# A hand-written plan with other keys, and the bias rows of two heads ahead of the rest in SP's queue

## The chip, the cores and the metric

The kernel runs on one core of one Trainium2 chip. The metric is the device time of one execution in microseconds (us); the time of a kernel is the median over its runs.

## The reference, cut to what matters

Three layers in a row: causal attention with a bias from a running sum, a dense layer that takes the largest of three products, and a layer that sends each token to one of 8 experts. The change touches the schedule of the first, with parts of the second in it.

```python
# attention: batch 4, heads 8, seq 576, head_dim 64
scores = scale * np.matmul(q, k.transpose(0, 1, 3, 2))
cum = np.cumsum(np.maximum(s, 0.0), axis=-1)
bias = -(cum[:, :, :, None] - cum[:, :, None, :])
scores = np.where(causal, -1000000000.0, scores + np.minimum(bias, 0.0))
attn = np.exp(scores - np.max(scores, axis=-1, keepdims=True))
attn = attn / (np.sum(attn, axis=-1, keepdims=True) + 1e-09)
x = np.matmul(attn, v)                       # -> 2304 tokens of 512
# dense: d_ff 768
h = np.maximum(np.maximum(x @ w1, x @ w2), x @ w3)
x = h @ w_out
# experts: 8 of 512 -> 1024 -> 512, the largest logit picks one
e_idx = np.argmax(x @ w_gate + modality_bias[modality_id], axis=1)
out[mask] = gate_w[mask, None] * (np.maximum(x[mask] @ w1[e], 0.0) @ w2[e])
```

## The kernel before, in words

The 32 heads go two by two (16 pairs, four pairs a batch, batch 1 first). Products in fp32 precision are made of parts: an operand is rounded to fp32r (its high part, `hl`, `xh`, `w_h`), what is left over is the low part (`q_b`, `xl`, `w_l`), and PE multiplies high with high and high with low.

What one head needs, in the order of its data:

- SP loads its queries and keys (L358, L359, job `lx`) and two rows of the running sum that PE adds as a bias (`lk`). For heads 0 and 1 these rows are read from the tile in SBUF where they are made (L373); for all others from a copy in DRAM (L375), which the job `rows` writes for all heads by two DMAs (L379).
- ACT rounds keys (L387, `ck`) and queries (L390, `cq`); POOL copies the keys (L393, `kb`) and makes the low parts (L397 `kl`, L400 `ql`). `ck` of heads 3 and 5 runs on POOL, `kl` of head 0 on DVE.
- PE makes the scores in six pieces (L407 and L408, `s`; 448, 320, 192 and 64 columns once each and 288 twice), each in one of 3 PSUM banks. DVE adds the mask and takes the minimum (L416, `mn`), ACT the exponentials (L423, `ex`), into one of 4 buffers.
- PE turns the 15 blocks of 128x128 (L428, `t`, four jobs), each in one of 2 PSUM banks; DVE or ACT copies them out (L433, `cp`).
- For each pair: ACT gathers the sums (L437, `r1`), DVE inverts them (L440, `r2`), PE turns them (L444, `rt`, in one of the same 2 banks), ACT copies them (L448, `rc`), SP writes them to DRAM and reads them back spread over partitions (L451, L456; `rw`, `rr`). PE multiplies by the values (L463, `pv`), DVE scales the result into x (L469, L473).

Between these go jobs of the dense layer. Nine of its weight blocks are loaded (L213, `wl`), decoded from float64 and split (L225 on ACT, `wz`; three steps on DVE, `w1`; a DMA issued by POOL, `wd`; a difference on POOL, `ws`). When a batch is done, its columns are split (L487 on ACT, `xc`; L491 on POOL, `xs`), and PE may do "fill" steps of three matmuls on them (L249 to L251, 288 columns, `f`; 168 steps in all). DVE and ACT copy their results (L502, L504, `fe`). The fills have the largest keys on PE: they run when nothing else can. What is left of them after the last head goes on beside the rest of the dense layer, whose matmuls of the same lines have 384 columns.

The order of all this is written out before the kernel is built: `planned` (L117) holds a list of jobs with estimated durations, buffers and transfer times. It takes for each engine the jobs that can start within `LOOK` = 60 ns of the soonest one, and of these the one with the smallest key; the engine with the earliest such start goes first. The keys come from the table `KEY` (L94): `at(h, what)` is h x T + KEY[what], so T is the distance between two heads. `n * KEY["ds"]` and `n * KEY["dt"]` keep the pieces of one head apart. `ready` is the earliest planned start, `wire` the planned time of a transfer and `land` what is added until its data is there. The jobs are then issued in the order found (`manual_schedule`), and each engine runs its own in that order. All that follows the attention is ordered by the compiler's own scheduler.

The lines that the change and its steps touch (the jobs `lk` of heads 0 and 1 stand in the diff, with key -2e8 + h; `kc` is the key of the split of a finished batch's part c, p being the batch's last pair):

```python
def at(h, what, n=0):
    return h * KEY["T"] + KEY[what] + n
rows = job("rows", rows_out, "SP", 1300, -1e8, after=[s_low_], wire=300)
kc = at(2 * (p - 3 + c) + 1, "xc")
```

Of the kernel before, what the change touches and what calls it, by code (L numbers as in the profile page):

```python
# [16 lines left out]
T = B * S  # L17
# [73 lines left out]
CONV = [(0, 3), (1, 3), (2, 5), (3, 7), (4, 7), (5, 9), (6, 13), (7, 15), (8, 17)]  # L91
W_READY, SET_H = 15000, 24
WIRE_FROM, WIRE_TO, WIRE_SLOW = 1300, 900, 1.0
KEY = {"s3": 262888, "T": 15750, "wl": 29386, "wz": 48740, "w1": 225687, "wd": 68498, "ws": 411529, "lx": 95995, "lv": 209700, "ck": 138477, "kb": -116340, "kl": -53033, "ql": -58361, "s": 115494, "mn": -5610, "ex": 153024, "ds": 361, "t": 18694, "dt": 19213, "cp": -53151, "r1": -208485, "r2": -212716, "rt": 15596, "rc": -242689, "rw": 44183, "pv": -165391, "x": -56845, "xc": 100720, "xs": -74110, "fe": -88191}  # L94
R_MOE1 = (2, 4, 7)
R_MOE2 = (1, 3, 5)

# [84 lines left out]
def fused_kernel(tc, qk, vd, sd, w64, mod, wg, wgt, mb, we, cst, csi, out):  # L182
    nc = tc.nc
    V, A, G, P, SP = nc.vector, nc.scalar, nc.gpsimd, nc.tensor, nc.sync
    top = ExitStack()
    with top:
# [73 lines left out]
        with ExitStack() as es:  # L260

            s3 = xbp.tile([32, 3, S], F32, tag="xb", name="s3")
# [83 lines left out]
            def job(name, run, eng, ns, key, **k):  # L346
                j = Job(run, eng, ns, key, **k)
                jobs.append(j)
                st[name] = j
                return j  # L350

            def at(h, what, n=0):
                return h * KEY["T"] + KEY[what] + n

            def load_x(h):
                p, j = divmod(h, 2)
                x = tl["x", h] = qkp.tile([128, 2, S], F32, name="qk_r", bufs=QR_BUFS)
                SP.dma_start(out=x[64:128, 1], in_=qk[PORD[p], 64:128, 1, j])  # L358
                (SP if h else A).dma_start(out=x[:, 0], in_=qk[PORD[p], :, 0, j])  # L359
                if h == 0:  # L360
                    SP.dma_start(out=mask[:, S - 128:S], in_=cst[:, 256:384])
                    SP.dma_start(out=ident, in_=cst[:, 0:128])

            def k_tile(h):
                if ("k_b", h) not in tl:
                    tl["k_b", h] = qkp.tile([66, S], F32R, name="k_b", bufs=KB_BUFS)
                return tl["k_b", h]

            def load_k(h):
                p, j = divmod(h, 2)  # L370
                k_b = k_tile(h)
                if p == 0:
                    SP.dma_start(out=k_b.bitcast(F32)[64:66], in_=augk.bitcast(F32)[16 * j + PORD[0]:16 * j + PORD[0] + 1])  # L373
                else:
                    SP.dma_start(out=k_b.bitcast(F32)[64:66], in_=dk[PORD[p], :, j])  # L375
# [5 lines left out]
            def values_in(p):  # L381
                v_r = tl["v_r", p] = vp.tile([128, 5, 128], F32, name="v_r")
                SP.dma_start(out=v_r, in_=vd[PORD[p]])

            def k_high(h):
                hl = tl["hl", h] = qkp.tile([128, 2, S], F32R, name="hl", bufs=HL_BUFS)
                (G.tensor_copy if h in CK_POOL else A.copy)(out=hl[64:128, 0], in_=tl["x", h][64:128, 1])  # L387
# [4 lines left out]
            def k_again(h):  # L392
                G.tensor_copy(out=k_tile(h)[0:64], in_=tl["x", h][64:128, 1])  # L393

            def k_low(h):
                hl = tl["hl", h]
                (V if h in KL_DVE else G).tensor_tensor(out=hl[0:64, 0], in0=tl["x", h][64:128, 1], in1=hl.bitcast(F32)[64:128, 0], op=ALU.subtract)  # L397

            def q_low(h):
                G.tensor_tensor(out=qbs[h % QB_N][0:64], in0=tl["x", h][0:64, 0], in1=tl["hl", h].bitcast(F32)[0:64, 1], op=ALU.subtract)  # L400
# [17 lines left out]
            def expo(h, c):  # L418
                p, j = divmod(h, 2)
                if ("l", p) not in tl:  # L420
                    tl["l", p] = ss.tile([128, 2, 5], F32, name="l")
                ec = e_bufs[h % E_N][:, EOFF[c]:EOFF[c] + QC[c][2]]
                A.activation(out=ec, in_=ec, func=ACTF.Exp, bias=tl["mn", h][:, c:c + 1], scale=-1.0, accum_out=tl["l", p][:, j, c:c + 1])  # L423
# [91 lines left out]
            sums_s = a = job("s2", s_sums, "DVE", 1346, -1e9, after=[a])  # L515
            b = job("s3", s_high, "ACT", 575, KEY["s3"], after=[a], ready=4350)
            a = job("s4", s_from, "DVE", 360, -1e9, after=[a], lock=True)
            s_low_ = job("s5", s_low, "DVE", 750, -1e9, after=[a, b], lock=True)
            rows = job("rows", rows_out, "SP", 1300, -1e8, after=[s_low_], wire=300)
            turns, highs = None, []  # L520
            for h in range(2 * NP):
                p, j = divmod(h, 2)
                s_x, s_k, s_h, s_q, s_e = (Slot(n) for n in ("qk", "kb", "hl", "qb", "e"))
                lx = job(("lx", h), lambda h=h: load_x(h), "SP", 1900 if h == 0 else 1130, at(h, "lx") if h > 2 else -1e9 + h, takes=[s_x], ready=750, wire=1700)
                if j == 0:
                    s_v, s_p, done = Slot("vr"), [], []
                    lv = job(("lv", p), lambda p=p: values_in(p), "SP", 430, at(h, "lv") if p else -9e8, takes=[s_v], wire=1300, ready=2000)
                ck = job(("ck", h), lambda h=h: k_high(h), "POOL" if h in CK_POOL else "ACT", 671 if h in CK_POOL else 640, at(h, "ck"), after=[lx], takes=[s_h], uses=[s_x], ready=4350)
                cq = job(("cq", h), lambda h=h: q_high(h), "ACT", 600, at(h, "ck", 1), after=[lx, ck], uses=[s_x, s_h])
                if h > 1:  # L530
                    lk = job(("lk", h), lambda h=h: load_k(h), "SP", 300 if h > 1 else 450, at(h, "lx", 1) if h > 1 else -2e8 + h, after=[rows], takes=[s_k], wire=100)
                kb = job(("kb", h), lambda h=h: k_again(h), "POOL", 657, at(h, "kb"), after=[lx, lk] if h > 1 else [lx], takes=[s_k] if h < 2 else [], uses=[s_x, s_k])
                if h < 2:
                    lk = job(("lk", h), lambda h=h: load_k(h), "SP", 300 if h > 1 else 450, at(h, "lx", 1) if h > 1 else -2e8 + h, after=[kb, s_low_], uses=[s_k], wire=100)
                kl = job(("kl", h), lambda h=h: k_low(h), "DVE" if h in KL_DVE else "POOL", 850 if h in KL_DVE else 1415, at(h, "kl"), after=[ck], uses=[s_x, s_h], lock=h in KL_DVE, tail=10 if h in KL_DVE else 0)
                ql = job(("ql", h), lambda h=h: q_low(h), "POOL", 1410, at(h, "ql"), after=[cq], takes=[s_q], uses=[s_x, s_h])
                ex = {}
                for n, (c, k) in enumerate(C_ORDER):
# [3 lines left out]
                    if k or c < 4:  # L542
                        ex[c] = job(("ex", h, c), lambda h=h, c=c: expo(h, c), "ACT", EXP_NS[c], at(h, "ex", n * KEY["ds"]), after=[a], uses=[s_e], tail=0)
                done += ex.values()
# [312 lines left out]
        for w in range(NW):  # L857
# [25 lines left out]
            for i in range(MW // 128):  # L883
                t = w * (MW // 128) + i
# [82 lines left out]
        at = unp.tile([128, U + 1], F32, name="at")  # L967
# [98 lines left out]
```

## Time and profile before

| | |
|---|---|
| median of 3 runs | 734.62 us (733.42 to 736.4) |
| the profiled execution | 734.0 us, its span 732.2 us |
| PE busy | 708.2 us, 97% |
| DVE busy | 497.4 us, 68% |
| ACT busy | 399.9 us, 55% |
| POOL busy | 225.3 us, 31% |

The span runs from the first to the last instruction; 1.8 us of the execution lie around it. PE's matmuls are pipelined and their ends are modelled, so the busy time of PE says that work was in it, not that it ran at its peak. The attention takes the first 210 us or so, and fills and the dense layer overlap its end; the shares above are means over stages with different limits.

### The profile page before, as it was taken

To read this page: it belongs to the slowest core of one execution; us is meant where nothing else is said; L and a number is where in the kernel's file an instruction comes from. 1 tells how busy PE (TensorE), PEld (TensorE's weight loads), DVE (VectorE), ACT (ScalarE), POOL (GpSimd) and SP (SyncE) were. 2 spreads that over 40 slices of the span, in tenths; PEclk is the share of its full clock that TensorE was granted. 3 is DMA by queue.
4 is the path that set the end of the run, shared out by engine and by line. 5 is a ranking of instruction groups with operands and counts; after the bars stand their busy time and mean duration, and the time that the engine had idled before them with its cause. 6 is when DMAs were issued, how large, how long until landed. Compare 5 with 4: busy or idle time off the path is not lost. (4 is left out here: it accounts for less than half of the span.)

```text
span 732.2 us, 13634 instructions
## 1 busy us (share of the span) xinstructions
PE 708.2 (97%) x4602; PEld 633.5 (87%) x4602; DVE 497.4 (68%) x1542; ACT 399.9 (55%) x984; POOL 225.3 (31%) x235
## 2 busy tenths in 40 slices
PE   4899999999999999999999999999999999999996
PEld 3677788878899899899999898999889988999884
DVE  5999787978667932673959796747775665565640
ACT  6899989898644511222222322636564765566631
POOL 8789868776101300010010101041421222212101
PEclk9999999999999999999999999999999999999999
DMA  7476666655236400101001101767567666666600
GB/s 214 144 219 188 203 184 212 190 151 147 81 127 209 164 26 6 49 1 31 36 23 54 52 21 51 258 159 247 153 214 265 225 208 220 212 224 226 222 35 19
DMA packets 43535, 103.83 MB, mean 142 GB/s; under 512 B 9472, under 2 KB 13472, under 8 KB 43456
## 3 DMA queue, kind: packets, MB, share of 16 engines
q1 hardware_dynamic: 35808, 86.04, 37.6%
q0 software_dynamic: 4912, 11.82, 5.1%
q10 hardware_dynamic: 2736, 5.01, 1.9%
q8 instruction: 38, 0.62, 0.4%
q14 instruction: 41, 0.34, 0.2%
HBM read 88.83 MB, written 12.18 MB: 138 GB/s over the span
## 5 line engine op out<-in xcount | busy, mean ns | idle before, releaser
L249 PE MATMUL a_ps<-xh,w_h 128*128 128x384 f32 (+2 forms) x492 | 159.4, 325 | 1.9 <-DVE h L504 1.1
L251 PE MATMUL a_ps<-xh,w_l 128*128 128x384 f32 (+2 forms) x492 | 155.8, 318 | 0.0
L250 PE MATMUL a_ps<-xl,w_h 128*128 128x384 f32 (+2 forms) x492 | 155.7, 317 | 0.0
L768 DVE TENSOR_TENSOR e_l<-e_raw,e_h 128x512 fp32r<-128x512 f32 x160 | 103.9, 689 | 13.5 <-ACT e_h L767 12.1
L767 ACT CAST e_h<-e_raw 128x512 fp32r<-128x512 f32 x160 | 92.9, 622 | 15.9 <-DMA e_raw<-in_we 6.9
L249 PEld LDWEIGHTS a_ps<-xh,w_h 128*128 128x128 f32 x492 | 92.6, 188 | 3.8 <-DVE h L504 1.4
L423 ACT ACTIVATE e<-e,mn 128x448 f32<-128x448 f32 (+4 forms) x160 | 88.6, 557 | 8.5 <-DVE mn L416 8.1
L250 PEld LDWEIGHTS a_ps<-xl,w_h 128*128 128x128 f32 x492 | 92.7, 188 | 0.3
L676 POOL DMA_INDIRECT table<-meta,si x18 | 19.6, 1088 | 238.1 <-DVE nm L664 83.2
L251 PEld LDWEIGHTS a_ps<-xh,w_l 128*128 128x128 f32 x492 | 92.4, 188 | 0.1
L798 PE MATMUL h_ps<-x2t,e_h 128*128 128x256 f32 x288 | 81.0, 282 | 0.0
L799 PE MATMUL h_ps<-x2t,e_l 128*128 128x256 f32 x288 | 80.9, 282 | 0.0
L797 PE MATMUL h_ps<-x2t,e_h 128*128 128x256 f32 x288 | 80.5, 282 | 0.0
L651 DVE CUSTOM_DVE_ANT_0 junk<-x,wg 128x512 bf16<-128x512 f32 x96 | 65.8, 686 | 17.2 <-ACT x L729 16.3
L407 PE MATMUL s_ps<-hl 128*128 128x288 f32 (+1 forms) x192 | 66.0, 354 | 9.9 <-DVE hl L397 6.9
L428 PE MATMUL t_ps<-ident,e 128*128 128x128 f32 x480 | 70.1, 280 | 1.4 <-DVE pt L433 0.6
L416 DVE CUSTOM_DVE_ANT_0 e<-s_ps,mask 128x288 f32<-128x288 f32 (+4 forms) x160 | 63.4, 424 | 9.5 <-PE s_ps L408 9.1
L827 PE MATMUL y_ps<-e_h,gh 128*128 128x512 f32 x152 | 61.5, 405 | 0.4 <-ACT gh L819 0.4
L408 PE MATMUL s_ps<-k_b,q_b 66*128 66x288 f32 (+1 forms) x192 | 57.9, 317 | 4.1 <-DMA k_b<-augk 3.9
L428 PEld LDWEIGHTS t_ps<-ident,e 128*128 128x128 f32 x480 | 56.0, 143 | 5.7 <-DVE pt L433 2.0
L829 PE MATMUL y_ps<-e_h,gl 128*128 128x512 f32 x152 | 60.7, 400 | 0.0
L828 PE MATMUL y_ps<-e_l,gh 128*128 128x512 f32 x152 | 60.0, 395 | 0.0
(179 smaller groups left out, 1484.0 us busy)
## 6 DMA issues: line engine op xcount, KB each, us to landing
e_raw<-in_we SPq DMA_DIRECT2D x80, 512.0 KB
w_raw<-in_w SPq DMA_DIRECT2D x24, 512.0 KB
qk_r<-in_qk SPq DMA_DIRECT2D x31, 288.0 KB
v_r<-in_vd SPq DMA_DIRECT2D x16, 320.0 KB
rb<-r_d SPq DMA_DIRECT2D x32, 160.0 KB
qk_r<-in_qk SPq DMA_DIRECT2D x32, 144.0 KB
x2d<-x ACTq DMA_DIRECT2D x18, 256.0 KB
w_h<-w_z POOLq DMA_DIRECT2D x9, 256.0 KB, 3.9
```

Of the source, the lines that this page charges most:

```text
L249: P.matmul(a_ps, wh[:, c], xh, start=c == 0, stop=False)
L250: P.matmul(a_ps, wh[:, c], xl, start=False, stop=False)
L251: P.matmul(a_ps, wl[:, c], xh, start=False, stop=c == 3)
L407: P.matmul(s_ps, hl[:, 1, q0:q0 + 128], hl[:, 0, k0:k0 + n], start=True, stop=False)
L423: A.activation(out=ec, in_=ec, func=ACTF.Exp, bias=tl["mn", h][:, c:c + 1], scale=-1.0, accum_out=tl["l", p][:, j, c:c + 1])
L428: P.transpose(out=t_ps[:, n * 128:(n + 1) * 128], in_=e_bufs[h % E_N][:, EOFF[c] + kb * 128:EOFF[c] + (kb + 1) * 128], identity=ident)
L651: V.tensor_tensor_reduce(out=junk, in0=x2, in1=wg_sb[ei // 2][:, ei % 2, :], scale=1.0, scalar=0.0, op0=ALU.mult, op1=ALU.add, accum_out=l ...
L767: A.copy(out=h, in_=raw[:, a])
L768: V.tensor_tensor(out=lo, in0=raw[:, a], in1=h.bitcast(F32), op=ALU.subtract)
L797: P.matmul(h_ps, w(hs, f, c), xt[:, 0, c], start=c == 0, stop=False)
L798: P.matmul(h_ps, w(hs, f, c), xt[:, 1, c], start=False, stop=False)
L799: P.matmul(h_ps, w(ls, f, c), xt[:, 0, c], start=False, stop=c == 3)
```

## The change

The diff is three lines. The first gives `KEY` other numbers (a result of a search by annealing, with other weights in what it looks for). The second lets the two writes of all heads' rows to DRAM start at 8500 ns of the plan at the earliest. The third adds 700 ns to the planned landing of the rows of heads 0 and 1. No instruction is added, removed or changed; the order on the engines and queues may differ.

```diff
-KEY = {"s3": 262888, "T": 15750, "wl": 29386, "wz": 48740, "w1": 225687, "wd": 68498, "ws": 411529, "lx": 95995, "lv": 209700, "ck": 138477, "kb": -116340, "kl": -53033, "ql": -58361, "s": 115494, "mn": -5610, "ex": 153024, "ds": 361, "t": 18694, "dt": 19213, "cp": -53151, "r1": -208485, "r2": -212716, "rt": 15596, "rc": -242689, "rw": 44183, "pv": -165391, "x": -56845, "xc": 100720, "xs": -74110, "fe": -88191}
+KEY = {"s3": -97664, "T": 7000, "wl": 40053, "wz": -18589, "w1": 32737, "wd": -43995, "ws": 98173, "lx": -66595, "lv": -5637, "ck": -4681, "kb": -52279, "kl": 21128, "ql": 9680, "s": -4267, "mn": -4185, "ex": 13414, "ds": 50, "t": 10767, "dt": 50, "cp": -42063, "r1": -6337, "r2": -61094, "rt": -71579, "rc": 7287, "rw": -3704, "pv": -70498, "x": -40039, "xc": 39659, "xs": -51512, "fe": 6144}
...
-            rows = job("rows", rows_out, "SP", 1300, -1e8, after=[s_low_], wire=300)
+            rows = job("rows", rows_out, "SP", 1300, -1e8, after=[s_low_], wire=300, ready=8500)
...
-                    lk = job(("lk", h), lambda h=h: load_k(h), "SP", 300 if h > 1 else 450, at(h, "lx", 1) if h > 1 else -2e8 + h, after=[kb, s_low_], uses=[s_k], wire=100)
+                    lk = job(("lk", h), lambda h=h: load_k(h), "SP", 300 if h > 1 else 450, at(h, "lx", 1) if h > 1 else -2e8 + h, after=[kb, s_low_], uses=[s_k], wire=100, land=700)
```

## Rows read from the trace of the kernel before

**Rows 1.** Windows: start:end and length, each engine's busy us, granted clock, DMA.

```profile
core 0: us, PE busy (x) PEld busy (x) DVE busy (x) ACT busy (x) POOL busy (x), PEclk, DMA share, GB/s
20.00:40.00 20.00, 17.54 (x123) 13.71 (x121) 18.97 (x63) 16.87 (x53) 16.70 (x15) 1.00 0.50 140
40.00:80.00 40.00, 38.79 (x290) 30.44 (x290) 36.69 (x124) 38.72 (x114) 34.67 (x33) 1.00 0.73 208
...
40.00:80.00 40.00, 14.01 (x96) 10.50 (x94) 1.00 0.73 208
```

The last of these rows is the same view of line L428 alone.

**Rows 2.** PE by shape, 20 to 80 us: count, busy us, mean ns, idle before.

```profile
L428 PE MATMUL t_ps<-ident,e 128*128 128x128 f32 x144 | 21.7, 280 | 1.3 <-DVE pt L433 0.6 <-ACT r_t L448 0.5
...
L463 PE MATMUL o_ps<-pt,v_r 128*64 128x512 f32 x20 | 5.4, 618 | 0.0
L407 PE MATMUL s_ps<-hl 128*128 128x448 f32 x11 | 4.7, 423 | 0.0
...
L249 PE MATMUL a_ps<-xh,w_h 128*128 128x288 f32 x7 | 2.1, 295 | 0.0
```

**Rows 3.** Timeline of PE, 190 to 222 us: start us, us, instruction, count.

```profile
191.24 0.47 PE L407 MATMUL s_ps<-hl 128*128 128x448 f32 x1
...
191.75 0.30 PE L407 MATMUL s_ps<-hl 128*128 128x288 f32 x1
...
192.05 0.39 PE L407 MATMUL s_ps<-hl 128*128 128x320 f32 x1
...
192.43 0.30 PE L249 MATMUL a_ps<-xh,w_h 128*128 128x288 f32 x1
...
192.83 1.04 PE L428 MATMUL t_ps<-ident,e 128*128 128x128 f32 x8
193.63 0.34 PE L407 MATMUL s_ps<-hl 128*128 128x192 f32 x1
...
194.07 0.38 PE L249 MATMUL a_ps<-xh,w_h 128*128 128x288 f32 x1
...
209.63 2.81 PE L463 MATMUL o_ps<-pt,v_r 128*64 128x512 f32 x20
...
212.49 0.41 PE L249 MATMUL a_ps<-xh,w_h 128*128 128x288 f32 x1
```

**Rows 4.** Timeline, SP's issues of the bias rows.

```profile
8.04 0.75 SPq L373 DMA_DIRECT2D k_b<-augk  x1
...
8.84 1.31 SPq L379 DMA_DIRECT2D dk<-augk  x2
...
10.20 0.64 SPq L373 DMA_DIRECT2D k_b<-augk  x1
```

**Rows 5.** Timeline, the first bias matmuls of heads 0 and 1.

```profile
11.42 0.58 PE L408 MATMUL s_ps<-k_b,q_b 66*128 66x288 f32 x1 [3.89 <-DMA k_b<-augk]
...
14.82 0.44 PE L408 MATMUL s_ps<-k_b,q_b 66*128 66x288 f32 x1
```

**Rows 6.** Timeline, head 3: its queries on ACT and POOL, its first matmul.

```profile
21.88 0.66 ACT L390 CAST hl<-qk_r 128x576 fp32r<-128x576 f32 x1
...
22.61 1.42 POOL L400 TENSOR_TENSOR q_b<-qk_r,hl 64x576 fp32r<-64x576 f32 x1 [4.74 <-ACT hl L390]
...
24.48 0.38 PE L407 MATMUL s_ps<-hl 128*128 128x288 f32 x1
```

**Rows 7.** Timeline, PE and its weight loads around a change of their duration.

```profile
16.82 1.91 PE L428 MATMUL t_ps<-ident,e 128*128 128x128 f32 x8
...
20.14 0.33 PEld L408 LDWEIGHTS s_ps<-k_b,q_b 66*128 66x128 f32 x1
...
20.96 0.19 PEld L407 LDWEIGHTS s_ps<-hl 128*128 128x128 f32 x1
```

**Rows 8.** Fill steps: by shape 205 to 300, window of L249 alone, timeline of ACT.

```profile
L249 PE MATMUL a_ps<-xh,w_h 128*128 128x288 f32 x104 | 31.8, 306 | 1.8 <-DVE h L504 1.1 <-ACT h L502 0.7
...
20.00:100.00 80.00, 5.78 (x19) 3.60 (x19) 1.00 0.65 186
...
72.31 0.77 ACT L487 CAST xh<-x 128x288 fp32r<-128x288 f32 x2
```

## The prediction, made before the result was known

> **What bounds the kernel now.** I read the windows first [rows 1], then the PE rows by shape in the stretch that looked short of work [rows 2], then single rows of the order of time [rows 3 to 7]. The busy column says that PE is nearly always busy, but that column counts each matmul until its modelled end, so I counted work instead: the time from one start to the next where PE is fed without a break [rows 3]. There one head's scores are 0.81 us (191.24 to 192.05: the shapes of 448 and 288 columns, with the small turn of a pair's sums in it), 0.30 for the second 288 (as 191.75 to 192.05), 0.38 for 320 (192.05 to 192.43) and 0.44 for 192 and 64 (193.63 to 194.07): 1.93 us. Eight transposes are 0.80 us (192.83 to 193.63), so the 15 of a head are 1.50. The values of a pair are 2.86 us (209.63 to 212.49), 1.43 a head. One fill step (three matmuls of the MoE layer on a finished half batch) is 0.40 us (192.43 to 192.83). A head is thus 4.86 us of PE.
>
> From 20 to 80 us PE did [rows 2] 11 heads of scores (the shape of 448 columns comes once a head), 144 transposes, 5 pairs of values (that of 512 columns comes four times a pair) and 7 fill steps: 21.2 + 14.4 + 14.3 + 2.8 = 52.7 of 60 us. PE lacks 7.3 us of work there. What is short is not PE: from 40 to 80 us ACT is busy 38.72 of 40 us, with 96 transposes, 6.4 heads, which makes 6.0 us of ACT a head; from 20 to 40 us DVE is busy 18.97 of 20 and ACT 16.87 [rows 1]. Fill steps are the cure, but they need a finished pair, so there are few: 19 by 100 us [rows 8]. After the last head's transposes at about 209 us PE has fills in stock, 104 of 168 steps start after 205 us, and all their waits there make 1.8 us, for the DVE and ACT copies of their results [rows 8]. So an order that feeds PE early takes fills out of that tail one for one, and an order that merely ends the heads sooner is worth nothing. From 260 us on nothing in the code is changed. The whole stock to be won is therefore 7.3 + 1.8, about 9 us of 732, and a bad order can cost as much.
>
> **The change, part by part.** No instruction is added or removed. The planner picks, among jobs that can start within 60 ns of the soonest one on an engine, the one with the lowest key; a job's key is head x T + its offset. Divided by T, the offsets say how many heads one kind of job may be ahead of another.
>
> 1. ACT, conversion against exponentials. Before, the query conversion of head 3 has key 3 x 15750 + 138477 + 1 = 185,728, behind the exponentials of heads 0, 1 and 2 (153,024, 168,774, 184,524). After, it has 3 x 7000 - 4681 + 1 = 16,320, behind head 0's (13,414) and ahead of head 1's (20,414). In general conversions go from level with the exponentials to 2 heads in front (offsets 8.8 against 9.7 heads before, -0.7 against 1.9 after). The row of it: ACT converts head 3's queries at 21.88, POOL had waited 4.74 us for that, and PE's first matmul of head 3 is at 24.48 [rows 6]. It will come some 4 to 5 us sooner. Worth between 0 and those 4.7 us. I take 1.0: DVE must take the minimum of those scores, and it has 20 - 18.97 = 1.03 us free from 20 to 40 us [rows 1], so that is the nearer row.
>
> 2. PE, transposes against scores. Before, every transpose goes ahead of any ready score (offsets 1.2 to 4.8 heads against 7.3). After, scores of heads up to 2 further on go ahead (1.54 against -0.61). Running ahead, 1.34 us of ACT (two conversions of some 0.67, as [rows 6] has one at 0.66) opens 1.93 us of PE. At the average of a head, 6.0 us of ACT for 4.86 of PE, 1.34 us of ACT opens only 1.09. Each head of lead is so worth 0.84 us, and two of them 1.7, once, and only while PE is short. It is bounded by 0 (the three buffers of converted operands or the four score buffers don't allow more lead) and 2 x 1.93 = 3.9 (ACT has the time anyway). I take 1.7: ACT at 38.72 of 40 hasn't the time.
>
> 3. ACT, preparing the fills. The split of a finished batch's columns for the fills (xc) had a key below the exponentials of all heads from 4 on (7 x 15750 + 100,720 = 210,970 for the fourth part); after, 7 x 7000 + 39,659 = 88,659, it stands behind the exponentials up to head 10 (83,414). In the trace two such splits run at 72.31 [rows 8], where ACT, at 6.0 us a head from about 16 us on, is near head 9 or 10 (an estimate). So it comes a head or so later, 6.0 us, while PE lacks 7.3 / 60 = 12%: 0.7 us lost. Bounds: 0, and all 19 steps by 100 us gone, 7.6 us. I take 0.7, since nearly all the steps still find room before the heads end.
>
> 4. The copy of the turned sums (rc) falls from 15 heads ahead of everything on ACT to about one ahead of its own head's exponentials, behind one or two conversions, 0.7 to 1.3 us; it holds one of two transpose banks meanwhile, and the reciprocals' way through DRAM starts that much later. PE has scores to run, so 0; without that cover 16 pairs x 0.7 = 11. The weight conversions' steps on DVE now go ahead of minima some 5 heads on instead of 15; those heads come past 60 us, where most are done: 0, bounded by one such step (0.7 us) either way.
>
> 5. The bias rows. The row asked first, head 0's, is issued at 8.04 behind its producer either way; PE waits for its landing until 11.42. `ready=8500` lets head 1's row, issued at 10.20 behind the two writes at 8.84 (1.31 us), go in front: some 1.3 us sooner [rows 4]. But head 1's first bias matmul runs at 14.82, right behind head 0's last one [rows 5], so 0 is gained; that queue of scores is the cover, and without it the row would be worth at most 1.3. The two writes, and the loads of heads 3 and 4 queued behind them on SP, move by the 0.6 us of the issue at most; head 2's rows are read from what they write. Bounded by 0.6 us lost, taken as 0, since head 3's operands already lay waiting for ACT [rows 6]. `land=700` changes only the plan: it then puts head 0's first full scores 0.7 us later, which is nearer the trace. It has no device time of its own.
>
> The sum: -1.0 - 1.7 + 0.7 = -2.0 us. The profiled execution is 734.0 us with a span of 732.2; so 732.0 for it, and as the median of the runs is 0.6 above it, **732.6 us**.
>
> **The clock of PE.** A weight load takes 0.33 us at 20.14 and 0.19 at 20.96, which are the levels of 1.2 and 2.4 GHz, although the granted clock of that stretch reads 1.00 [rows 1, 7]. Ahead of the rise PE did scores, then from 16.82 transposes among scores [rows 7]. "TensorE: Matmul & The Clock Gate" (the Trainium skill, Part 4: PE-mode transpose) says that transposes don't count as activity for that clock. By that rule scores in front of transposes would bring the rise forward; it is rival D, and no row here tells how much of the time before 20.14 hangs on it.
>
> **The rivals.**
> A. *Most of the shortage goes* (20%): the lead of two heads also removes DVE's starts and stops, the tail's waits vanish, and PE gets 5 of 7.3 us and 1 of 1.8 back: 734.6 - 6 = 728.6. For it: POOL and ACT waited for each other early [rows 6]. Against: ACT and DVE are nearly full where PE is short [rows 1].
> B. *The fills come too late* (23%), slower than before. xc sits behind the exponentials, so PE meets the stretch from 60 to 100 us without stock. It decides when fill steps done by 100 us fall from 19 to about 9 or fewer: then 10 x 0.40 = 4 us move into the full tail, with no gain left to set against it but a part of 1 and 2: 738.6. All 19 gone would be 742.2.
> C. *Another order, the same bounds* (17%): with ACT and DVE full, no order between them changes what PE gets; the bias rows are hidden. 734.6, give or take 1.
> D. *The clock rises sooner* (4%): with scores in front, PE would have the high level from 16.82 on and not from about 20.5 [rows 7]; at most these 3.7 us are halved, 1.8 on top of the forecast: 730.8.
>
> **How the numbers follow.** Forecast 36%, A 20%, B 23%, C 17%, D 4%. A measurement of this kernel tells about 0.5%, 3.7 us, from no change: faster is below 730.9, slower above 738.3. The forecast spreads some 3 us to each side (a quarter of it below 730.9), A nearly all faster, B four fifths slower, C all within, D half. Faster 0.09 + 0.20 + 0.02 = 0.31; slower 0.19, and 0.02 taken from the forecast for a stall I don't see, 0.21; within 0.48. The range of 726.8 to 739.2 takes in A with a further 2 us, and B up to just past its middle; the forecast's own range is 729.6 to 735.6.
>
> **What would show it.** Right: head 3's first scores before 21 us; from 20 to 80 us more than 52.7 us of counted work, with 12 or 13 heads of scores beside no fewer transposes; fewer than 104 fill steps after 205 us, by about 5. Step 5: the row of head 1 issued at about 8.8, PE's first bias matmul still at 11.4. Wrong: scores run ahead but the transposes and values of 20 to 80 us fall by as much (then part 2 is empty); under 15 fill steps by 100 us (part 3 was too cheap, B); PE waiting on the copied sums (part 4); or a change of time after 260 us, where the code is the same.

## The result, and the profile after

The changed kernel is slower: its median is 739.92 us (739.19 to 742.19, 6 runs), that of the kernel before in the same comparison 737.08 (733.42 to 738.41, 6 runs). These two medians are 2.8 us apart; the ratio of the runs is put at 1.0059, with an interval of 1.004 to 1.0079: some 4.4 us, where 2.0 us less was forecast. The fastest of the six, 739.19, lies above every run of the kernel before that was taken beside it or beside the experiments, the slowest of which is 738.5. The profiled execution took 739.65 us, its span 737.7, against 734.0 and 732.2 before: 5.65 us more, of which a part is that the execution profiled before was one of its kernel's faster ones.

To find these microseconds I counted for each matmul of PE the time from its start to the next start, less the usual spacing of its shape (the median over the kernel before). What is left over is time that PE lost, to waits or to its lower clock. Sums in us, for this pair and for the experiments further on:

| kernel | 0–20 | 20–120 | 120–160 | 160–220 | 220–260 | to 300 | ratio to before |
|---|---|---|---|---|---|---|---|
| before | 7.7 | 5.6 | -0.3 | 2.6 | 2.9 | 18.9 | 1 |
| after | 6.6 | 4.9 | 4.9 | 1.0 | 6.4 | 24.2 | 1.0059 |
| e1_swap | 6.1 | 7.5 | -0.5 | 2.6 | 3.0 | 19.2 | 0.9998 |
| e2_after_fe | 6.9 | 4.8 | 4.8 | 1.0 | 5.6 | 23.5 | 1.0048 |
| e3_keys | 7.2 | 8.3 | 3.1 | 1.7 | 5.0 | 25.7 | 1.0107 |
| e4_rows | 7.0 | 8.0 | 2.2 | 1.2 | 3.4 | 22.2 | 1.0041 |
| e5_ck_behind | 6.6 | 5.9 | 3.2 | 1.0 | 5.1 | 22.1 | 1.0038 |
| e6_after_split | 6.5 | 5.0 | 4.5 | 1.0 | 1.2 | 18.5 | 0.9989 |
| e7_after_turns_first | 7.2 | 13.3 | 2.1 | 1.1 | 5.9 | 31.4 | 1.0147 |
| e8_before_ex | 7.0 | 5.1 | 6.1 | 6.8 | 2.5 | 27.9 | 1.0146 |
| e9_before_split | 6.9 | 8.1 | -0.5 | 2.7 | 2.0 | 19.7 | 1.0003 |
| e10_after_both | 6.7 | 5.9 | 4.4 | 1.1 | 0.9 | 19.4 | 0.9995 |
| e11_after_xc | 6.7 | 7.1 | 4.9 | 1.6 | 4.2 | 24.8 | 1.007 |
| e12_pool_beside | 6.8 | 4.8 | 4.3 | 1.2 | 5.1 | 22.6 | 1.006 |

Up to 120 us the new order gains 1.8 us; from 120 to 160 it loses 5.3, from 160 to 220 it gains 1.6, and from 220 to 260 it loses 3.5. Behind 260 us nothing differs between the two by more than 0.2. The sum, +5.3 at 300 us, accounts for the 5.65.

The windows of the kernel after show the same places (start:end and length, busy us of each engine, granted clock, DMA); the first stands beside [rows 1]:

```profile
20.00:40.00 20.00, 18.23 (x122) 13.62 (x122) 19.88 (x71) 19.06 (x58) 16.15 (x15) 1.00 0.49 149
...
120.00:160.00 40.00, 36.72 (x275) 28.41 (x275) 34.13 (x108) 35.95 (x103) 30.89 (x27) 1.00 0.62 171
...
230.00:235.00 5.00, 3.79 (x28) 3.52 (x26) 4.96 (x7) 1.58 (x4) 3.78 (x4) 1.00 0.66 215
235.00:240.00 5.00, 3.46 (x17) 3.47 (x18) 4.49 (x9) 2.71 (x5) 0.00 (x0) 0.75 0.51 157
...
250.00:255.00 5.00, 3.65 (x25) 3.18 (x25) 3.50 (x4) 1.19 (x3) 3.17 (x3) 1.00 0.14 49
```

And two of the kernel before, where PE had been full:

```profile
120.00:160.00 40.00, 39.95 (x315) 32.89 (x316) 32.19 (x117) 37.03 (x110) 31.29 (x30) 1.00 0.65 186
230.00:240.00 10.00, 10.00 (x70) 9.92 (x69) 9.51 (x19) 5.19 (x9) 0.00 (x0) 1.00 0.68 220
```

PE's busy time falls where POOL (the last engine ahead of the clock) works: 3.78 of 5 us from 230 to 235 and 3.17 from 250 to 255, where the kernel before has 0.00 and 0.54. From 235 to 240 the granted clock falls to 0.75. The timeline of the kernel after (start us, us, instruction, count, idle time before it and what ended it), POOL, DVE, ACT and PE in turn, tells how:

```profile
229.41 4.38 POOL L491 TENSOR_TENSOR xl<-x,xh 128x288 fp32r<-128x288 f32 x4 [26.26 <-ACT xh L487]
...
228.62 0.42 DVE L227 TENSOR_SCALAR w_z<-w_z 128x512 int32<-128x512 int32 x1
...
229.64 1.31 DVE L229 SCALAR_TENSOR_TENSOR w_z<-w_raw,w_z 128x512 int32<-128x512 int32 x1
230.87 0.45 DVE L504 TENSOR_TENSOR h<-a_ps,h 128x288 f32<-128x288 f32 x1
231.23 0.93 DVE L231 SCALAR_TENSOR_TENSOR w_z<-w_raw,w_z 128x512 int32<-128x512 int32 x1
232.08 1.03 DVE L227 TENSOR_SCALAR w_z<-w_z 128x512 int32<-128x512 int32 x1
233.15 1.18 DVE L229 SCALAR_TENSOR_TENSOR w_z<-w_raw,w_z 128x512 int32<-128x512 int32 x1
...
236.13 0.69 DVE L229 SCALAR_TENSOR_TENSOR w_z<-w_raw,w_z 128x512 int32<-128x512 int32 x1
...
234.96 0.67 ACT L225 ACTIVATE w_z<-w_raw 128x512 f32<-128x512 f32 x1 [2.15 <-DVE w_l L238]
235.57 0.62 ACT L236 CAST w_h<-w_z 128x512 fp32r<-128x512 f32 x1
236.09 0.39 ACT L502 COPY h<-a_ps 128x288 f32<-128x288 f32 x1
...
236.54 0.40 PE L249 MATMUL a_ps<-xh,w_h 128*128 128x288 f32 x1 [2.75 <-ACT h L502]
...
238.35 0.44 PE L250 MATMUL a_ps<-xl,w_h 128*128 128x288 f32 x1
238.59 0.44 PE L251 MATMUL a_ps<-xh,w_l 128*128 128x288 f32 x1
...
253.22 0.40 PE L250 MATMUL a_ps<-xl,w_h 128*128 128x288 f32 x1 [1.26 <-POOL xl L491]
```

POOL splits the columns of the next half batch (four in a row, 4.38 us). Beside it, DVE's steps in decoding weights (L229, L231, L227) take 1.31, 0.93, 1.03 and 1.18 us instead of 0.69, 0.69, 0.42 and 0.69: 1.96 us in all. ACT's two weight steps wait for DVE (2.15 us), the copy of a fill's result (L502) stands behind them on ACT, and PE, which needs that bank, waits 2.75 us. Then its matmuls of 288 columns start 0.24 us apart (238.35 to 238.59), nearly twice their usual spacing of 0.13, which is the level of 1.2 GHz, until 240.75. The second burst, around 250 us, costs in another way: there PE waits 1.26 us, at 253.22, for a split of POOL itself. In the kernel before only one such burst of four lay in this stretch, and cost waits of 1.12 and 0.52:

```profile
242.70 4.18 POOL L491 TENSOR_TENSOR xl<-x,xh 128x288 fp32r<-128x288 f32 x4 [20.35 <-ACT xh L487]
```

The decoding here is not of the plan's nine blocks, whose `w_l` POOL makes: DVE makes it here (L238), in code that follows the attention's and that the compiler's scheduler has placed between the plan's jobs. So the plan holds POOL's splits of the tail, and not the DVE steps that they meet.

The other place, from 150 to 157 us (SP, ACT and PE in turn):

```profile
151.52 0.48 SPq L358 DMA_DIRECT2D qk_r<-in_qk  x1
...
154.92 0.67 ACT L387 CAST hl<-qk_r 64x576 fp32r<-64x576 f32 x1 [1.85 <-DMA qk_r<-in_qk]
155.62 0.56 ACT L423 ACTIVATE e<-e,mn 128x320 f32<-128x320 f32 x1
156.08 0.19 ACT L423 ACTIVATION_READ_ACCUMULATOR e<-e,mn 128x1 f32 x1
156.18 0.35 ACT L433 COPY pt<-t_ps 128x256 f32<-128x256 f32 x1
...
156.58 0.66 PE L428 MATMUL t_ps<-ident,e 128*128 128x128 f32 x4 [1.57 <-ACT pt L433]
```

ACT's conversion of head 28's keys was planned ahead of a copy of transposes. Its operands, asked at 151.52, came late; ACT waited 1.85 us for them with the copy behind it, and PE 1.57 us for the copy's bank.

### The profile page after: what moved, and what is told of

It reads as the page before. It is cut to its first block, busy times and chain, and to the rows that moved or that the text cites. A ratio compares the mean times of both kernels' runs of the same rounds, so it can differ in the third digit from the quotient of the medians.

```text
span 737.7 us, 13665 instructions
## 1 busy us (share of the span) xinstructions
PE 709.6 (96%) x4602; PEld 633.8 (86%) x4602; DVE 504.0 (68%) x1542; ACT 399.2 (54%) x984; POOL 229.2 (31%) x235
## 5 line engine op out<-in xcount | busy, mean ns | idle before, releaser
L249 PE MATMUL a_ps<-xh,w_h 128*128 128x384 f32 (+2 forms) x492 | 159.0, 324 | 2.9 <-ACT h L502 2.8
L249 PEld LDWEIGHTS a_ps<-xh,w_h 128*128 128x128 f32 x492 | 93.2, 190 | 4.1 <-ACT h L502 3.3
L676 POOL DMA_INDIRECT table<-meta,si x18 | 19.7, 1093 | 237.1 <-DVE nm L664 83.1
L428 PE MATMUL t_ps<-ident,e 128*128 128x128 f32 x480 | 69.7, 279 | 3.9 <-ACT pt L433 2.1
L428 PEld LDWEIGHTS t_ps<-ident,e 128*128 128x128 f32 x480 | 54.8, 142 | 10.1 <-ACT pt L433 4.7
```

Of the source, the lines that this page charges most:

```text
L249: P.matmul(a_ps, wh[:, c], xh, start=c == 0, stop=False)
L428: P.transpose(out=t_ps[:, n * 128:(n + 1) * 128], in_=e_bufs[h % E_N][:, EOFF[c] + kb * 128:EOFF[c] + (kb + 1) * 128], identity=ident)
```

## The experiments

No experiment leaves work out or changes what is computed; only e12_pool_beside adds some. The ratio is always to the kernel before, with its interval.

**e1_swap.** The kernel before, with the row of head 1 asked ahead of the two writes, by hand, so that nothing else moves:

```diff
-sequence = planned(jobs)
+sequence = planned(jobs); sequence.remove(rows); sequence.insert(sequence.index(st["lk", 1]) + 1, rows)
```

> The kernel before, with one thing moved: in SP's queue the two writes of the rows to DRAM go behind head 1's bias row instead of ahead of it; all other engines keep their order word for word. Theory: the row is not waited for (PE reaches head 1's bias matmul at 14.8 us, behind head 0's), so the time is that of before within 0.3%; head 1's row is issued near 8.8 and PE still starts at 11.4. Rival: the writes delay head 0's row while it is on its way, and PE starts about 0.5 us sooner. Rival: the writes, now later, hold up the loads of heads 3 and 4 and cost 0.6 us or more.

Measured: 735.47 us, 0.9998 (0.9984 to 1.0012). The earlier row is worth nothing that these runs can tell, about 1 us either way.

**e3_keys** and **e4_rows.** One half of the change each: the new table `KEY` alone, and the two other lines alone with the old table.

```diff
 e3_keys, against the kernel before
-KEY = {"s3": 262888, "T": 15750, ...}
+KEY = {"s3": -97664, "T": 7000, ...}
 e4_rows, against the kernel after
-KEY = {"s3": -97664, "T": 7000, ...}
+KEY = {"s3": 262888, "T": 15750, ...}
```

> The new keys alone, with the old planned times of the rows. The planner finds another order from it than for the changed kernel from the first heads on, though by the same preferences. Theory (the preferences do it, fills late): fewer than 15 fill steps by 100 us and under 50 by 200 us, as in the changed kernel (14 and 46 there by the count of its matmuls), and 0.4 to 0.8% slower than before. Rival (one unlucky order): the preferences don't matter, and this order's time lies anywhere within 0.6% of before, with its waits at other places.

> The old keys with the two planned times of the rows changed (writes from 8500 ns, rows landing 700 ns later). The device gains nothing from the rows themselves, but the planner finds another order from the second head on. Theory: fills keep their old place in the order (about 19 steps by 100 us, 60 by 200 us), and the time is that of before within 0.4%. Rival (one unlucky order): anywhere within 0.8%, with waits at other places, since a plan made for other times is no longer tuned.

Measured: 743.42 us, 1.0107 (1.009 to 1.0124) for the keys, and 737.77, 1.0041 (1.0025 to 1.0057) for the two lines. The halves, +7.9 and +3.0 us, don't add up to the whole, +4.4. The two lines, whose device effect is nothing (e1_swap), cost 3 us through the plan alone: with them the planner draws another order of everything behind. The planner knows a part of this itself. Run alone, without the chip, it ends its last job at 243.8 us for the kernel before, at 246.2 for e3_keys and 245.7 for e4_rows, but at 243.4 for the kernel after, which it takes to be the best of the four.

**e2_after_fe.** The first theory for the tail: PE waits because the copy of a fill stands on ACT behind weight steps; so put these copies on DVE.

```diff
-A.copy(out=tl["h", i, f], in_=a_ps)
+(V.tensor_copy if i in (0, 1, 4, 5, 6, 7) else A.copy)(out=tl["h", i, f], in_=a_ps)
```

> The changed kernel with one edit: in the fills of the batches done last (halves 4 to 7) the copy of the first product runs on DVE instead of ACT. The attention's order stays, instruction by instruction, up to the end of the heads; only the tail behind about 200 us differs. Theory (tail): PE's wait of 2.75 us at 236 us for that copy, which stands on ACT behind a weight conversion that waits for DVE, and the low clock of PE after it (0.75 granted from 235 to 240 us) are most of the loss; without them the kernel is 3 to 4.5 us faster than the changed one, so within 0.3% of before, and the granted clock is 1.00 from 225 to 250 us. Rival (attention): the loss is the waits of PE for bank copies from 120 to 160 us (4.9 us there); then the edit leaves 0.4 to 0.8% above before.

Measured: 739.4 us, 1.0048 (1.0031 to 1.0065), and 5.6 us still lost from 220 to 260. Which engine copies is not the cause: DVE is where the delay arises, and the copies now stand behind it there.

**e6_after_split** and **e9_before_split.** The second theory: the splits on POOL and the decoding on DVE slow each other. The splits of the half batches of the tail go to DVE, in both kernels.

```diff
 e6_after_split, against the kernel after
-G.tensor_tensor(out=tl["xl", i, c], in0=xb[b][:, c, o:o + FW], ...)
+(V if i in (0, 1, 5, 6, 7) else G).tensor_tensor(out=tl["xl", i, c], in0=xb[b][:, c, o:o + FW], ...)
 e9_before_split, against the kernel before
-G.tensor_tensor(out=tl["xl", i, c], in0=xb[b][:, c, o:o + FW], ...)
+(V if i > 5 or i == 5 and c > 1 else G).tensor_tensor(out=tl["xl", i, c], in0=xb[b][:, c, o:o + FW], ...)
```

> The changed kernel with the low parts of the last three half batches (5 to 7) for the fills made on DVE instead of POOL; the attention's order stays. In the changed kernel POOL makes four of them from 229.4 to 233.8 us, DVE's decoding steps beside it take 0.9 to 1.3 us instead of 0.4 to 0.7, and PE waits 2.75 us at 236.5 and 1.3 at 253. Theory (the borders between half batches in the tail, where POOL and DVE slow each other): PE's waits from 225 to 255 us fall from 4.2 to under 2.5 us, and the kernel is 1.5 to 3 us faster than the changed one, a ratio to before of 1.002 to 1.004. Rival (DVE is full in the tail whoever makes them, and any work on it is paid in full): the waits move to other places and their sum stays at 4 to 6 us; ratio 1.005 to 1.007.

> The kernel before with the same edit as the changed one had in the run named after the split: the low parts for the fills of the halves behind the last head (6, 7 and the second half of 5) on DVE instead of POOL; the attention's order stays. Theory (POOL and DVE slow each other at the borders between half batches in the tail, and that is a loss of its own in either kernel): PE's lost time from 220 to 260 us falls from 2.9 to about 1, and the time by 1.5 to 2.5 us, a ratio of 0.997 to 0.998. With it the two attentions can be compared without their tails: before is then 1 to 2 us faster than the changed kernel with the same edit (0.9989). Rival (before's tail loses for another reason, the result copies behind the decoding): no change, 1.000.

Measured: 734.52 us, 0.9989 (0.9974 to 1.0003) on the kernel after; its whole loss is gone, 6.4 us lost from 220 to 260 become 1.2. On the kernel before 736.01, 1.0003 (0.9985 to 1.0022): there the one burst cost little, 2.9 become 2.0, and the 1.5 to 2.5 us that I expected didn't come. With the splits on DVE in both, the two kernels take the same time: what the change costs in the end is the tail. Two rows of e6_after_split, one window and the splits on DVE:

```profile
230.00:240.00 10.00, 9.87 (x72) 9.45 (x70) 9.93 (x22) 5.09 (x10) 0.00 (x0) 1.00 0.57 190
...
230.32 1.19 DVE L491 TENSOR_TENSOR xl<-x,xh 128x288 fp32r<-128x288 f32 x3
```

Three splits in a row take DVE 1.19 us, about 0.4 each, where POOL took 1.1. That leaves two readings: the decoding was slowed, or the splits were merely late.

**e12_pool_beside.** To part them: as e6_after_split, and POOL makes the same differences again, for nobody. They are 12 (235 instructions of POOL instead of 223), and not 20 as I had written.

```diff
 against e6_after_split, behind the line of the split
+i in (0, 1, 5, 6, 7) and G.tensor_tensor(out=tl["idle"]..., in0=xb[b][:, c, o:o + FW], ...)
```

> The splits of the later half batches stay on DVE, and POOL makes the same differences once more into a tile that nobody reads: 20 operations of POOL are added, no result changes. Theory (POOL reading beside DVE slows the decoding, and that alone brings the waits back): DVE steps of 128x512 beside the spare differences take 1.0 to 1.3 us instead of 0.69, PE loses 3 to 6 us from 220 to 260 us instead of 1.2, and the ratio to the kernel before is 1.003 to 1.007. Rival (the splits were simply late on POOL, each some 1.1 us instead of 0.45): nobody waits for the spare differences, PE's loss from 220 to 260 us stays under 2 us, and the ratio stays at 0.998 to 1.001.

Measured: 740.43 us, 1.006 (1.0041 to 1.008), with 5.1 us lost from 220 to 260. Rows of its timeline and two windows:

```profile
228.56 4.10 POOL L491 TENSOR_TENSOR idle__3155<-x,xh 128x288 fp32r<-128x288 f32 x4 [25.74 <-ACT xh L487]
...
228.72 1.30 DVE L229 SCALAR_TENSOR_TENSOR w_z<-w_raw,w_z 128x512 int32<-128x512 int32 x1
229.95 1.06 DVE L491 TENSOR_TENSOR xl<-x,xh 128x288 fp32r<-128x288 f32 x1
230.94 0.44 DVE L504 TENSOR_TENSOR h<-a_ps,h 128x288 f32<-128x288 f32 x1
231.30 2.04 DVE L491 TENSOR_TENSOR xl<-x,xh 128x288 fp32r<-128x288 f32 x3
...
230.00:240.00 10.00, 8.79 (x59) 7.81 (x59) 9.93 (x19) 3.84 (x7) 2.50 (x3) 1.00 0.45 148
245.00:255.00 10.00, 8.59 (x61) 7.81 (x60) 9.53 (x16) 3.80 (x9) 3.94 (x4) 1.00 0.24 79
```

Work that feeds nothing brings the whole loss back. DVE's step of 128x512 takes 1.30 us, three splits 2.04 instead of 1.19, and both windows in which POOL works lose PE time again, with no loss of clock. POOL beside DVE is the cause. Late splits are part of the way, not a rival to it: of PE's two longest waits here one is for the copy behind the decoding (0.78 us at 234.95), as in the kernel after, and one for a split (0.95 at 248.75), late because it was slowed on DVE.

**e5_ck_behind** and **e10_after_both.** The place at 156 us: head 28's key conversion and the split of its keys go right behind the copies of transposes; then both this and the splits on DVE.

```diff
-sequence = planned(jobs)
+sequence = planned(jobs); late_ = [st["ck", 28], st["kl", 28]]; sequence = [j for j in sequence if j not in late_]; i_ = sequence.index(st["cp", 22, 2]) + 1; sequence[i_:i_] = late_
```

> The changed kernel with one instruction moved: on ACT the key conversion of head 28 goes behind the exponential of 320 columns and the bank copy of 256 that stand behind it. All other engines keep their order up to the late expert stage. In the changed kernel that conversion held ACT for 1.85 us for a load, the two copies waited behind it, and PE waited 1.57 us for one of them at 156.6 us. Theory (PE's waits before the tail count in full, and come from work that the plan put in front and that isn't ready): the wait at 156 us goes, PE's lost time from 120 to 160 us falls by some 1.5 us, and the kernel is 1 to 2 us faster than the changed one, a ratio to before of 1.003 to 1.005. Rival (the fills take up any gap, and only the tail counts): the wait moves elsewhere, and the ratio stays at 1.006.

> The changed kernel with both edits that made it faster: head 28's key conversion behind the two instructions that it held up, and the late splits on DVE. Theory (PE's lost times add up): 1.5 us for the one and 5 us for the other, 733 us, a ratio to before of 0.996 to 0.998. Rival (the one gap is taken by what the other opened): 0.998 to 1.000, as with the splits alone.

Measured: 738.59 us, 1.0038 (1.0022 to 1.0054), with 3.2 us lost from 120 to 160 instead of 4.9. Its interval overlaps that of the kernel after, so that this place counts in the end is likely, but not shown. Both together: 734.82, 0.9995 (0.9976 to 1.0014), no better than the splits alone. In that profile the wait is back, two microseconds on:

```profile
158.40 0.98 PE L428 MATMUL t_ps<-ident,e 128*128 128x128 f32 x7 [1.24 <-ACT pt L433]
```

**e7_after_turns_first.** The kernel after with transposes again ahead of all ready scores.

```diff
-KEY = {..., "s": -4267, ...}
+KEY = {..., "s": 49330, ...}
```

> The changed kernel with one key put back to its old place in heads: scores at 7.05 heads (49330) instead of -0.6, so that transposes go ahead of scores again. It tests part 2 of the prediction alone. Theory (running scores ahead does feed PE early, as predicted): PE loses some 2 us more than the changed kernel up to 120 us, and the time is 2 to 5 us above the changed one, a ratio to before of 1.009 to 1.013. Rival (scores ahead of transposes are what starves the fills, 14 of them by 100 us): more fill steps by 100 us (16 or more), and the time at or below the changed kernel's, a ratio of 1.006 or less.

Measured: 746.9 us, 1.0147 (1.0116 to 1.0177). From 20 to 120 us PE loses 13.3 us, where the kernel after loses 4.9. The plan, too, ends later, at 248.8 us.

**e8_before_ex.** The kernel before with one key moved by 3 hundredths of the distance between two heads, which the plan holds to be as good (243.8 us planned to the end of its jobs before, 244.1 with it).

```diff
-KEY = {..., "ex": 153024, ...}
+KEY = {..., "ex": 153500, ...}
```

> The kernel before with the key of the exponentials raised by 0.03 heads (153024 to 153500): the preferences are the same to all purposes, but the order on the engines differs from the first few heads on, and the planned end moves by 0.3 us only. It tells how far the time scatters between orders that the plan holds for equal. Theory (the change is slower because of what its new preferences do): the same as before within 0.25%. Rival (before is one lucky draw, picked among many such orders, and nearly any other is slower): 0.3 to 0.8% slower, with PE waiting 2 to 5 us more in places that differ from those of the changed kernel.

Measured: 745.92 us, 1.0146 (1.0117 to 1.0175), the loss from 140 to 200 us. Its two largest waits:

```profile
146.21 0.66 PE L428 MATMUL t_ps<-ident,e 128*128 128x128 f32 x4 [1.81 <-DVE pt L433]
...
180.83 1.02 PE L428 MATMUL t_ps<-ident,e 128*128 128x128 f32 x4 [3.06 <-DVE x L473]
```

A change of no meaning costs more than the change under study. Three orders that the plan holds equal within 0.7 us (before, after and this one) lie some 10 us apart on the chip.

**e11_after_xc.** The kernel after with the split of finished columns (xc) ahead of the exponentials again.

```diff
-KEY = {..., "xc": 39659, ...}
+KEY = {..., "xc": -9900, ...}
```

> The changed kernel with the key of the fills' preparation put ahead of the exponentials again, 3.3 heads as before (xc from 39659 to -9900). It tests part 3 of the prediction. Prediction's own step: fills come about one head earlier and 0.7 us is won back (1.004 to 1.006). Rival (what keeps fills out is that PE has heads' work instead, not that they aren't ready): fill steps by 100 us stay at 13 or 14, and the time moves only as any new order does, by anything from -2 to +6 us, with the difference in waits that have nothing to do with fills.

Measured: 740.99 us, 1.007 (1.0051 to 1.0089), and 13 fill steps by 100 us, as without it. Its plan ends at 246.4 us.

## Why the prediction was wrong, by its own steps

**Part 1** has its size about right, but the sign that I named for it failed and its reason is not shown. ACT converted head 3's queries at 16.07 us instead of 21.88 [rows 6], yet its first scores came only 0.87 us sooner, at 23.61 instead of 24.48, and not before 21. DVE is busy 19.88 of 20 us from 20 to 40, as the part argued from 18.97 [rows 1], but PE waited for its minima only 0.19 us ahead of those scores; it had head 2's scores and transposes to do until then. So that 0.87 lies near the 1.0 that I took may be luck.

```profile
16.07 0.66 ACT L390 CAST hl<-qk_r 128x576 fp32r<-128x576 f32 x1
...
20.89 0.40 PE L407 MATMUL s_ps<-hl 128*128 128x288 f32 x1 [0.19 <-DVE mn L416]
...
23.61 0.38 PE L407 MATMUL s_ps<-hl 128*128 128x288 f32 x1
```

**Part 2** has the right direction, as far as one order can tell, and its size is not shown. The PE rows by shape from 20 to 80 us, against [rows 2]:

```profile
L428 PE MATMUL t_ps<-ident,e 128*128 128x128 f32 x138 | 19.9, 277 | 0.5 <-ACT r_t L448 0.2
...
L463 PE MATMUL o_ps<-pt,v_r 128*64 128x512 f32 x20 | 5.4, 618 | 0.6 <-ACT pt L433 0.6
L407 PE MATMUL s_ps<-hl 128*128 128x448 f32 x12 | 4.8, 402 | 0.0
...
L249 PE MATMUL a_ps<-xh,w_h 128*128 128x288 f32 x8 | 2.6, 320 | 0.0
```

One head's widest scores more and one fill step more, but 6 transposes fewer, where I had asked for no fewer. With each matmul counted at its usual spacing, as in the table, the window holds 54.9 us of work against 54.1; e6_after_split, with the same order up to there, has 54.4. A gain of 0.3 to 0.8 us is hardly told from none. To 120 us there is a gain: the six profiles with this order up to 120 us (after, e2, e5, e6, e10, e12) lose 11.5 to 12.6 us by then, the three with the order before (before, e1, e9) 13.3 to 15.0; the means differ by 2.0. That this equals the forecast's -2.0 for parts 1 to 3 is luck, as far as these runs tell: e3_keys, with the same keys and so the same preferences, loses 15.5 us to 120, and e8_before_ex, with the old ones, 12.1. In e7_after_turns_first, without the lead, PE loses 8.4 us more to 120 us, and the time is some 6.5 us longer (1.0147 against 1.0059), beyond the bound of 3.9. It is one order among others that scatter, but its 13.3 us from 20 to 120 lie outside all the rest (4.8 to 8.3). I had priced the lead by heads, and PE's waits without it, for DVE's minima (3.1 us) and for the bank that holds a part of x until DVE has scaled it (2.1 us), were not in that price.

**Part 3** fell, in its reason and in its price. Fill steps by 100 us did drop, from 19 to 13, under the 15 that I had named as a sign of being wrong, and 116 instead of 104 start after 205 us [rows 8], where I expected some 5 fewer:

```profile
20.00:100.00 80.00, 4.21 (x13) 2.47 (x13) 1.00 0.68 194
...
L249 PE MATMUL a_ps<-xh,w_h 128*128 128x288 f32 x116 | 35.1, 303 | 2.8 <-ACT h L502 2.8
...
71.05 0.78 ACT L487 CAST xh<-x 128x288 fp32r<-128x288 f32 x2
```

But the key of xc is not why: the splits that run at 72.31 us in the kernel before [rows 8] run at 71.05 here and not a head later, and with the old place of the key there are still 13 (e11_after_xc). PE had heads' work to do instead: from 20 to 100 us, each matmul at its usual spacing, 70.4 us of it against 66.9, and 5.2 us of fills against 7.5. And it costs nothing that shows: e6_after_split has the same 13 and 116 and takes no longer than the kernel before. That fills move into the tail "one for one" is true only of time that PE would have lost; a fill that gives way to a head is no loss.

**Part 4** holds: PE waited 0.2 us in all for copied sums from 20 to 80 us, in the row of 138 transposes above.

**Part 5** holds for the transfers and fails for the plan. SP issues both rows first, and PE starts at 11.30 and 14.70, against 11.42 and 14.82 [rows 4, 5]:

```profile
8.29 1.41 SPq L373 DMA_DIRECT2D k_b<-augk  x2
9.74 1.30 SPq L379 DMA_DIRECT2D dk<-augk  x2
...
11.30 0.58 PE L408 MATMUL s_ps<-k_b,q_b 66*128 66x288 f32 x1 [3.45 <-DMA k_b<-augk]
...
14.70 0.44 PE L408 MATMUL s_ps<-k_b,q_b 66*128 66x288 f32 x1
```

e1_swap puts its device time at nothing. But "it has no device time of its own" was read as no cost, and e4_rows shows 3.0 us from these two lines by the order that the plan then draws; 1.9 of them stand in the plan itself.

**The step that failed** is the sum itself. It named the stock, 7.3 us early and 1.8 in the tail, and said that a bad order can cost as much; then it had terms only up to 100 us, and took all that lies behind, which the new keys order anew, at nothing without a reason. From 120 to 160 us the kernel before loses nothing and in the tail 2.9 us: a well placed order, with everything to lose there and nothing to win. The terms that were missing are +5.3, -1.6 and +3.5 us, against -1.8 where I looked. The one price that the prediction had for decoding on DVE is part 4's, one step of the plan's own blocks, 0.7 us; that of the tail had none, and beside one burst of POOL's splits it lost 1.96 us, and PE waited 2.75. The tail's part is shown by e6_after_split and e12_pool_beside: bursts of POOL's splits beside DVE's decoding. The part at 120 to 160 us is shown in its place (e5_ck_behind), but not as a cause by itself: the gaps change place from order to order.

**The rivals.** A, most of the shortage goes: no. B ended on the right side, by the wrong way: 13 steps lie between its 9 and 19, and not the fills' place but POOL's splits at the borders between half batches cost the time. C, the same bounds, give or take 1 us: no; e8_before_ex lies 10 us from the order that it hardly differs from in its keys. D: the weight loads do shorten sooner, to 0.23 at 18.95 and 0.19 at 19.10 instead of 20.96 [rows 7], but that needs no new order: e1_swap, with the PE order of before, has 0.19 at 17.92. So no run here shows whether transposes count for the clock.

```profile
17.92 0.19 PEld L407 LDWEIGHTS s_ps<-hl 128*128 128x128 f32 x1
...
18.95 0.23 PEld L407 LDWEIGHTS s_ps<-hl 128*128 128x128 f32 x1
19.10 0.19 PEld L408 LDWEIGHTS s_ps<-k_b,q_b 66*128 66x128 f32 x1
```

## What to carry to other kernels

Where an order is drawn by a planner, a change of its keys, or of a number that only the plan knows, is a new draw of everything behind it; price it by the scatter between orders that the plan holds equal (here some 10 us, from three orders), and not by the one stretch whose mechanism you can follow. Run the planner first: the four orders that it put 1.9 to 5.0 us later were 3.0 to 11 us slower. All six new orders drawn here were slower than the one before (1.0041 to 1.0147), so that one looks like a good draw. Ask of each stretch how much PE loses now: where it loses nothing, a new order can only lose. And look for two engines that slow each other where the plan holds one of them only: to take POOL's splits from beside the decoding was the only cure found here, though no version was clearly faster than the kernel before.

## What the runs showed of the hardware

**POOL and DVE.** Beside POOL's differences from SBUF, DVE's steps with two operands in SBUF take 1.30 us instead of 0.69 (128x512), and the splits of 128x288 1.06 instead of 0.45, three in a row 2.04 instead of 1.19. POOL is slowed too: some 1.1 us a split in the bursts of four, 0.80 for one at 199.28 in e6_after_split. L504, which takes one operand from PSUM, keeps its 0.45 (230.87 in the kernel after, 230.94 in e12_pool_beside). "SBUF — State Buffer" (the Trainium skill, Who interferes with whom) says that a DVE instruction with two SBUF inputs contends with a GpSimd instruction that reads SBUF; these rows agree. L227, with a single operand from SBUF, is a case that this sentence doesn't name, and it was slowed as well: 1.03 us at 232.08 instead of 0.42.

**PE's clock.** With one and the same order on PE, the moment at which weight loads fall from 0.33 to 0.19 us lay at 20.96 in the kernel before and at 17.92 in e1_swap. The early rise was lost again: behind a wait of 2.27 us that ended at 30.57 (1.44 at 31.26 in the kernel before) the granted clock of e1_swap fell in the next 10 us, and that of the kernel before didn't:

```profile
30.00:40.00 10.00, 9.09 (x45) 8.27 (x45) 9.00 (x33) 8.09 (x26) 8.70 (x9) 0.66 0.51 142
```

From 20 to 120 us e1_swap lost 7.5 us, the kernel before 5.6. In the tail the same is seen the other way: after its 2.75 us wait the kernel after fell to 0.75, while e2_after_fe, whose wait in that place was 1.70 us, ending at 236.39, kept 1.00 and took about as long (1.0048). Between executions of one kernel the clock tells more: of the 22 of the kernel before beside e9_before_split, the six with a mean granted clock of 0.998 or 0.999 took 733.19 to 734.61 us, the six with 0.990 to 0.992 took 736.18 to 738.5. Between the kernels before and after it tells little: its median is 0.994 over those 22 and 0.9935 over the six of the kernel after.
